# Decode attention, two gated branches on one core: one loop per engine for both branches, with branch A's sums folded and dealt out after the loops

## The chip, the core and the metric

One core of one Trainium2 chip runs the program. The metric is the device time in microseconds (us) of one execution, as the median of several runs. The engines are named as in the profile: PE (matmuls, with PEld for its weight loads), DVE (vector), ACT (scalar activations), POOL, and SP, whose queue issues nearly all the transfers of this kernel.

## What is computed

Two attention branches A and B, each with its own query weights, caches and output weights, are applied to the same `x` (two batches, one token, 512 wide) and mixed by a sigmoid gate. Each branch has 32 heads of 128 and a cache of 4096 tokens, all in float32.

```python
def _A_ref(x, k_cache, v_cache, wq, wo):        # B, Sq, D = 2, 1, 512; Hq = Hkv = 32; Sk = 4096; Dh = 128
    q = (x @ wq).reshape(B, Sq, Hq, Dh).transpose(0, 2, 1, 3)
    scores = einsum("bhqd,bhkd->bhqk", q, k_cache) * Dh ** -0.5
    p = softmax(scores, axis=-1)
    o = einsum("bhqk,bhkd->bhqd", p, v_cache)
    return o.transpose(0, 2, 1, 3).reshape(B, Sq, Hq * Dh) @ wo
...
g = sigmoid((x * gate_w).sum(-1, keepdims=True))
return g * A_ref(x, ...) + (1 - g) * B_ref(x, ...)
```

The four caches are 134 MB each and are read once. With both `wq` and both `wo` (8.4 MB each) this makes the 570 MB that the program reads.

## The kernel before

The work is cut into 32 **units**, first 16 of A and then 16 of B: a unit is four heads (a group `g` of eight) of one batch `b`. A unit's keys fill one tile of 128 partitions x 128 rows x 128 values (8.4 MB), its values another. There are two key tiles, `kt[0]` for even and `kt[1]` for odd units, and one value tile `vt`. Those three nearly fill the on-chip memory.

**Transfers.** All of them stand in SP's queue in one fixed order (L515 to L526): both `wq`, keys 0 and 1, values 0, then keys u and values u-1 in turn, then `wo` of A (into `kt[0]`), the last unit's values in three parts, and `wo` of B (into `kt[1]`) in six parts. A key transfer waits for `k_free`, which DVE gives once it has reduced the unit before in that tile (L395); a value transfer waits for `v_free`, which ACT gives once PE has used the values before (L432, L457).

**Each unit.** DVE multiplies the key tile by the spread query (L391) and reduces it to scores (L394), takes the maximum over each head (L399 to L401) and spreads the next query (L404, L405). ACT makes the exponentials (L365) into the padded weights `pr`, and their sums, one column per unit, into `lp`. PE multiplies them with the value tile (L369; 32 matmuls, which the profile shows as 64 records, since each float32 matmul is there twice). The output `vp` gathers both batches of a group. After the second unit, ACT and DVE fold its four strips into `vs[:, g]` (L452, L415), and ACT clears `vp` (L459).

**Loops and the seam between the branches.** DVE, ACT and PE each have their own loop. Before the change each runs through a loop for A, then a stretch of straight code, then a loop for B. In the straight code, the *seam*, DVE folds A's sums (`sum_of`, L467 to L470: transpose `lp`, reduce, reciprocal, times the gate), PE gathers A's eight `vs` pieces into `heads` (L473), ACT scales that into `vs[:, 0]` (L478), PE deals it out with the matrix `deal` (L482, eight matmuls) and ACT copies the result into `onA` (L485). In `deal_out`, ACT does this ahead of the exponentials of B's first unit. `deal` itself is a tile of its own, built from the identity matrix at the program's start (L313 to L320).

**The end.** After its B loop, PE projects A through `wo` of A into `most` (L497, 32 matmuls), gathers the first seven `vs` pieces of B, multiplies the last unit's weights with its values as their three parts land (`last_products`, L598), gathers the last piece, and deals B out. It then projects B, 28 rows into `most` and the last four into `qa` (L512), and adds `most` to them (L612). POOL and DVE build a second identity and a folding matrix for this in `kt[0]`, once PE has read `wo` of A there (L589 to L592). Two copies each on DVE and ACT and two small transfers end the program (L616 to L624).

PE, DVE, ACT and POOL run their instructions in the order of the code. The helper `put` adds the waits: an instruction waits for those that wrote what it reads, and for those that read or wrote what it writes. PE doesn't wait for itself.

Of the kernel before, what the change touches and what calls it, by code (L numbers as in the profile page):

```python
# [7 lines left out]
F32 = mybir.dt.float32  # L8
AF = mybir.ActivationFunctionType
# [11 lines left out]
NG = H // G  # L21
NS = SK // PH
# [119 lines left out]
def tile_gated_decode(ctx: ExitStack, tc: tile.TileContext, ins: dict, out: bass.AP):  # L142
# [9 lines left out]
    gate = {n: small.tile([P, 1], F32, name="gate" + n) for n in "AB"}  # L152
    padded = small.tile([P, NVC, B, G * VC], F32, name="pr")
    lp = small.tile([P, PH], F32, name="lp")
    slot = small.tile([P, VC], F32, name="slot")
    pick = small.tile([P, NG * B + P], F32, name="pick")
    deal = small.tile([P, B, DQ, NG, G, DQ], F32, name="deal")
    qcol = {n: small.tile([P, NG, DH // QT, B], F32, name="qcol" + n) for n in "AB"}
# [9 lines left out]
    nil = small.tile([P, 1], F32, name="nil")  # L168
# [10 lines left out]
    with tc.tile_critical():  # L179
# [10 lines left out]
        r_vs = [R() for _ in range(NG)]  # L190
# [122 lines left out]
        put("dve", lambda x: x.memset(deal, 0.0), [], [r_deal])  # L313
        for b in range(B):
            for k in range(DQ):
                piece = R()
                piece.writers = r_deal.writers[:1]
                vput("dve", lambda x: x.tensor_copy(deal[:, b, k, :, :, k], ident.rearrange(
                    "p (h g b) -> p b g h", h=G, b=B)[:, b, :NG]), [r_ident], [piece])
        r_deal.writers = piece.writers  # L320
# [4 lines left out]
        def project(n):  # L325
            i_k = place["wq", n]
            if n == "A":
                room, mark = Scratch(vt, 8 * P + D), lambda p: r_vt.readers.append(p)
            else:
                room, mark = Scratch(kt[i_k]), lambda p: None  # L330
            halves = kt[i_k].rearrange("p r d -> p (r d)").rearrange(
                "p (c i g h d) -> p c i h g d", c=KC, i=NG // STRIPS, h=G, d=DH)
            for i, t in enumerate(qa):
                put("dve", lambda x: x.memset(t, 0.0), [], [r_qa[i]])
            for c in range(KC):
                arrived("pe", ("wq", n), *((c * len(parts["wq", n]) // KC,)))
                for i, t in enumerate(qa):
                    for h in range(G):
                        put("pe", lambda x: x.matmul(t[h * QT:h * QT + B], cols[:, c], halves[:, c, i, h],  # L339
                                                     start=c == 0, stop=c == KC - 1), [r_cols, *r_kt[i_k]], [r_qa[i]])  # L340
# [10 lines left out]
            mark(put("dve", lambda x: x.tensor_copy(qcol[n], wide.rearrange("p (g k b) -> p g k b", g=NG, b=QT)[:, :, :, :B]),  # L351
                     [r_wide], [r_qcol[n]]))
            for r in r_kt[i_k]:
                r.readers += r_wide.readers

        def spread_queries(u):
            n, g, b = units[u]
            put("dve", lambda x: x.tensor_copy(qsel, qcol[n][:, g:g + 1, :, b:b + 1]), [r_qcol[n]], [r_qsel])
            put("dve", lambda x: x.transpose(q, qsel[:, 0].to_broadcast([P, DH // QT, QT])), [r_qsel], [r_q])
# [43 lines left out]
        def next_queries(n, g, b):  # L403
            at = D_.do(lambda x: x.tensor_copy(qsel, qcol[n][:, g, :, b:b + 1]))  # L404
            return D_.do(lambda x: x.transpose(q, qsel[:, 0].to_broadcast([P, DH // QT, QT])), at)  # L405

        def dve_second(nxt):
            take("dve", k_landed[1], 16)
            maxima_of(1, whole_scores(1, 0))
            return next_queries(*nxt, 0) if nxt else 0  # L410
# [7 lines left out]
        def dve_first(g, nxt, at, between=None):  # L418
# [4 lines left out]
            if between:  # L423
                between()
            maxima_of(0, at)
            next_queries(*nxt, 1)
# [27 lines left out]
        def act_first(g, col, between=None):  # L454
# [5 lines left out]
            if between:  # L460
                between()
# [3 lines left out]

        def sum_of(n):
            put("dve", lambda x: x.transpose(across, lp), [r_lp], [r_across])  # L467
            put("dve", lambda x: x.tensor_reduce(rs, across, axis=AX.X, op=ALU.add), [r_across], [r_rs])
            put("dve", lambda x: x.reciprocal(rs, rs), [], [r_rs])
            put("dve", lambda x: x.tensor_tensor(rs, rs, gate[n], op=ALU.mult), [r_gate[n]], [r_rs])  # L470

        def gather(g):
            put("pe", lambda x: x.matmul(heads, pick[:, (NG - g) * B:][:, :P], vs[:, g], start=g == 0, stop=g == NG - 1),  # L473
                [r_pick, r_vs[g]], [r_heads])

        def deal_out(n):
            t = vs[:, 0]
            put("act", lambda x: x.activation(t, heads, AF.Copy, scale=rs), [r_heads, r_rs], [r_vs[0]])  # L478
            dealt = bank[:, :B * OR].rearrange("p (b r) -> p b r", b=B)
            for b in range(B):  # L480
                for k in range(DQ):
                    put("pe", lambda x: x.matmul(dealt[:, b], deal[:, b, k].rearrange("p g h q -> p (g h q)"),  # L482
                                                 t[:, k * OR:(k + 1) * OR], start=k == 0, stop=k == DQ - 1),
                        [r_deal, r_vs[0]], [r_bank])
# [59 lines left out]
        def step(e, n, lo, hi, second, first):  # L544
            with nc.Fori(lo, hi, engines=[{"dve": mybir.EngineType.DVE, "act": mybir.EngineType.Activation}[e]]) as i:
                first(i, second(i))

        def dve_pairs(n):
            S.wait("dve", [*r_q.writers, (S.sems["dve"], S.ticks["dve"])])
            with nc.Fori(0, NG - 1, engines=[mybir.EngineType.DVE]) as i:  # L550
                nxt = n, bass.ds(i + 1, 1)
                at = dve_second(nxt)
                dve_first(i, nxt, at)

        def act_pairs():
            with nc.Fori(0, NG - 1, engines=[mybir.EngineType.Activation]) as i:
                act_second(bass.ds(i * B + 1, 1))
                act_first(i, bass.ds(i * B + B, 1))
# [23 lines left out]
        end = Scratch(kt[place["wo", "A"]]).take  # L582
        ident2, fold, onb, kept = end(P), end(QT), end(OR * B), end(D)
        totals = [end(D // OS)[:B].rearrange("b (s e) -> b s e", s=STRIPS // OS) for _ in range(OS)]
        on["B"] = onb.rearrange("p (r b) -> p r b", b=B)
        r_ident2, r_fold, r_kept, r_total = R(), R(), R(), [R(), R()]
        for r in (r_ident2, r_fold, r_kept, r_on["B"], *r_total):
            r.readers = [p for x in r_kt[place["wo", "A"]] for p in x.readers]
        put("pool", lambda x: x.memset(ident2, 0.0), [], [r_ident2])  # L589
        put("pool", lambda x: x.affine_select(out=ident2, in_=ident2, compare_op=ALU.not_equal, fill=1.0, base=0,  # L590
                                              pattern=[[-1, P]], channel_multiplier=1), [], [r_ident2])
        put("dve", lambda x: x.tensor_reduce(fold, ident2.rearrange("p (s q) -> p q s", s=STRIPS), axis=AX.X, op=ALU.add),  # L592
            [r_ident2], [r_fold])
# [5 lines left out]
        take_out(NG - 1)  # L599
        take("dve", taken)  # L600
        for a in range(1, VC):
            put("dve", lambda x: x.scalar_tensor_tensor(  # L602
                vs[:, NG - 1], vp[:, a * DH:(a + 1) * DH], slot[:, a:a + 1], vs[:, NG - 1], op0=ALU.mult, op1=ALU.add),
                [r_vs[NG - 1]] if a > 1 else [], [r_vs[NG - 1]] if a > 1 else [])
            r_vs[NG - 1].writers = [(S.sems["dve"], S.ticks["dve"])]
        gather(NG - 1)
        deal_out("B")
        project_out("B", EARLY)
        put("act", lambda x: x.activation(kept, most, AF.Copy), [r_most], [r_kept])  # L609
# [6 lines left out]
        for i, e in enumerate(("dve", "act")):  # L616
            for j in range(STRIPS // OS):
                k = (i * STRIPS // OS + j) * QT
                src = acc[i][k:k + B, :D // STRIPS]
                put(e, (lambda x: x.activation(totals[i][:, j], src, AF.Copy)) if i else  # L620
                    (lambda x: x.tensor_copy(totals[i][:, j], src)), [r_qa[i]], [r_total[i]])  # L621
            landed.append(S.dma("act" if i else "sp", out.rearrange("b o (i s e) -> (b o) i s e", i=OS, s=STRIPS // OS)[:, i],
                                totals[i], reads=[r_total[i]], slot="x"))
# [23 lines left out]
```

## Time and profile before

| | |
|---|---|
| time, median of 3 runs | 1324.59 us (1324.45 to 1324.62) |
| the profiled execution | 1324.58 us, with a span of 1322.8 us from first to last instruction |
| transfers | 570.43 MB read, mean 431 GB/s over the span |
| DVE | 1166.3 us busy, 88% of the span |
| PE | 343.3 us busy, 26%; mean granted clock 0.627 |
| ACT | 101.4 us busy, 8% |

Times in rows of the trace are in us from the span's start. A row of the timeline gives the start, the duration, the engine, the line and operation, what is written and read, and a count where instructions are merged. The square bracket says how long the engine had been idle before, and what ended that.

### The profile page before, as it was taken

What the parts mean: (1) busy time and instruction counts of PE and PEld (TensorE: products, weight loads), DVE (VectorE), ACT (ScalarE), POOL (GpSimd) and SP (SyncE); (2) the same over time, 40 slices, a digit from 0 to 9 for tenths busy, and PEclk for the clock granted to TensorE, in tenths of its full rate; (3) what the DMA queues carried; (4) which work ended last, traced back from release to release, by engine and by line L of the source; (5) the groups of instructions that cost most, each with busy time, mean ns of one, the idle gap of its engine ahead of it and who ended that gap; (6) DMA issues with size and microseconds to landing.
All of it is one profiled execution on the core that took longest, in us unless ns stands there. A gap on an engine that the chain in (4) does not pass through costs nothing. (4 is left out here: it accounts for less than half of the span.)

```text
span 1322.8 us, 6257 instructions
## 1 busy us (share of the span) xinstructions
PE 343.3 (26%) x2406; PEld 100.7 (8%) x2406; DVE 1166.3 (88%) x321; ACT 101.4 (8%) x331; POOL 1.2 (0%) x8
## 2 busy tenths in 40 slices
PE   3202222202222221222224022222212222221256
PEld 0000000000000000000002000000000000000012
DVE  2399999999999999999999899999999999999960
ACT  0000000001010000101000010100001010000100
POOL 0000000000000000000000000000000000000000
PEclk9656666556666655666665566666566666656668
DMA  9999999999999999999999999999999999999998
GB/s 412 442 414 442 442 416 442 444 414 444 442 430 428 442 442 416 442 442 416 444 442 419 438 442 434 426 440 440 420 440 440 420 442 442 426 432 442 434 420 357
DMA packets 11109, 570.53 MB, mean 431 GB/s; under 512 B 1239, under 2 KB 1243, under 8 KB 1630
## 3 DMA queue, kind: packets, MB, share of 16 engines
q1 hardware_dynamic: 11092, 570.43, 99.6%
q8 instruction: 4, 0.07, 0.0%
q14 instruction: 3, 0.02, 0.0%
q10 hardware_dynamic: 10, 0.01, 0.0%
HBM read 570.43 MB, written 0.00 MB: 431 GB/s over the span
## 5 line engine op out<-in xcount | busy, mean ns | idle before, releaser
L391 DVE TENSOR_TENSOR kt<-kt,q 128x16384 f32<-128x16384 f32 x31 | 534.0, 17226 | 56.1 <-DVEq L95 56.0
L394 DVE TENSOR_REDUCE sc<-kt 128x128 f32<-128x16384 f32 x31 | 533.8, 17220 | 1.1
L369 PE MATMUL vp<-vt,pr 128*32 128x512 f32 x2048 | 291.8, 733 | 919.3 <-PEq L95 918.5
L369 PEld LDWEIGHTS vp<-vt,pr 128*32 128x32 f32 x2048 | 80.3, 132 | 1129.3 <-issue 1126.9
L365 ACT ACTIVATE pr<-sc,nm 32x128 f32<-32x128 f32 x128 | 50.9, 398 | 160.0 <-ACTq L95 118.2
L431 ACT ACTIVATE pr<-nil 128x512 f32<-128x512 f32 x31 | 19.3, 624 | 426.4 <-ACTq L95 426.4
L452 ACT ACTIVATE vs<-vp,slot 128x128 f32 (+1 forms) x16 | 5.9, 368 | 451.6 <-ACTq L95 451.6
L339 PE MATMUL qa<-kt,cols 128*2 128x512 f32 x128 | 18.7, 741 | 22.9 <-DMA kt<-in_B_wq_dram 15.7
L365 ACT ACTIVATION_READ_ACCUMULATOR pr<-sc,nm (+1 forms) x128 | 23.5, 184 | 0.0
L350 DVE STREAM_TRANSPOSE kt<-kt 128x1024 f32<-128x1024 f32 x1 | 1.2, 1246 | 23.5 <-ACT kt L348 23.5
L415 DVE SCALAR_TENSOR_TENSOR vs<-vp,slot,vs 128x128 f32 (+1 forms) x45 | 15.8, 351 | 6.3 <-DVEq L95 5.3
L534 DVE TENSOR_REDUCE sc<-kt 128x64 f32<-128x8192 f32 x2 | 17.4, 8686 | 0.1
L533 DVE TENSOR_TENSOR kt<-kt,q 128x8192 f32<-128x8192 f32 x2 | 17.4, 8686 | 0.0
L459 ACT ACTIVATE vp<-nil 128x512 f32<-128x512 f32 x15 | 9.0, 600 | 106.6 <-ACTq L95 106.6
L621 DVE COPY kt<-qa 2x128 f32<-2x128 f32 x2 | 0.6, 280 | 17.0 <-PE qa L512 17.0
L592 DVE TENSOR_REDUCE kt<-kt 128x32 f32<-128x128 f32 x1 | 0.4, 368 | 12.8 <-POOL kt L590 12.8
L497 PE MATMUL most<-kt,onA 128*2 128x512 f32 x64 | 8.6, 698 | 9.5 <-DMA kt<-in_A_wo_dram 9.5
L399 DVE TENSOR_REDUCE rm<-sc 128x1 f32<-128x128 f32 x31 | 8.7, 282 | 2.3
L405 DVE STREAM_TRANSPOSE q<-qsel 128x128 f32<-128x128 f32 x30 | 9.3, 311 | 1.3 <-DVE qsel L404 0.3
L602 DVE SCALAR_TENSOR_TENSOR vs<-vp,slot,vs 128x128 f32<-128x128 f32 x3 | 1.1, 352 | 10.6 <-DVEq L95 10.6
L350 DVE STREAM_TRANSPOSE vt<-vt 128x1024 f32<-128x1024 f32 x1 | 1.2, 1246 | 9.4 <-ACT vt L348 9.4
L497 PE MATMUL most<-kt,kt 128*2 128x512 f32 x56 | 8.6, 779 | 2.4 <-DMA kt<-in_B_wo_dram 2.4
(68 smaller groups left out, 72.9 us busy)
## 6 DMA issues: line engine op xcount, KB each, us to landing
kt<-in_A_wq_dram SPq DMA_DIRECT2D x2, 4096.0 KB, 16.6
kt<-in_A_k_cache_dram SPq DMA_DIRECT2D x2, 4096.0 KB, 29.0
vt<-in_B_v_cache_dram SPq DMA_DIRECT2D x1, 4096.0 KB, 18.3
kt<-in_B_wo_dram SPq DMA_DIRECT2D x1, 4096.0 KB, 33.1
vt<-in_B_v_cache_dram SPq DMA_DIRECT2D x1, 3072.0 KB, 25.2
kt<-in_B_wo_dram SPq DMA_DIRECT2D x1, 2048.0 KB, 37.5
vt<-in_B_v_cache_dram SPq DMA_DIRECT2D x1, 1024.0 KB, 27.2
kt<-in_B_wo_dram SPq DMA_DIRECT2D x1, 1024.0 KB, 39.5
```

Source lines behind the costliest of these rows:

```text
L339: put("pe", lambda x: x.matmul(t[h * QT:h * QT + B], cols[:, c], halves[:, c, i, h], start=c == 0, stop=c == KC - 1), [r_cols, *r_kt[i_k]] ...
L365: do(lambda x: x.activation(padded[h, :, b, j * VC:(j + 1) * VC], s[h].rearrange("p (c a) -> p c a", a=VC), AF.Exp, bias=m[h], accum_out=l ...
L369: return x.matmul(vp[c % STRIPS * QT:(c % STRIPS + 1) * QT], padded[:, c].rearrange("p b m -> p (b m)"), vt[:, c * VC:(c + 1) * VC].rearra ...
L391: at = D_.do(lambda x: x.tensor_tensor(kt[o], kt[o], q[:, None, :].to_broadcast([P, NS, DH]), op=ALU.mult), after)
L394: at = D_.do(lambda x: x.tensor_reduce(sc[o], kt[o], axis=AX.X, op=ALU.add), at)
L405: return D_.do(lambda x: x.transpose(q, qsel[:, 0].to_broadcast([P, DH // QT, QT])), at)
L415: at = D_.do(lambda x: x.scalar_tensor_tensor(vs[:, g], vp[:, a * DH:(a + 1) * DH], slot[:, a:a + 1], vs[:, g], op0=ALU.mult, op1=ALU.add) ...
L431: return A_.do(lambda x: x.activation(padded[:, :, b], nil[:, :, None].to_broadcast([P, NVC, G * VC]), AF.Copy))
L459: A_.do(lambda x: x.activation(vp, nil.to_broadcast([P, VC * DH]), AF.Copy))
L497: put("pe", lambda x: x.matmul(most[s * QT:s * QT + B], on[n][:, r], wo[n][:, r], start=n == "A" and r < STRIPS, stop=n == "B" and r >= EA ...
L533: put("dve", lambda x: x.tensor_tensor(t, t, q[:, None, :].to_broadcast([P, NS // 2, DH]), op=ALU.mult), [r_q], [r])
L534: put("dve", lambda x: x.tensor_reduce(sc[0][:, h * NS // 2:(h + 1) * NS // 2], t, axis=AX.X, op=ALU.add), [r], [R()])
```

## The change

The two loops of each engine become one, over 15 of the 16 pairs of units; PE's runs 31 times. The straight code of the seam moves behind the loops. For this, `vs` holds 16 pieces instead of 8, so that A's sums stay unfolded until the end. `qcol` becomes one tile for both branches, so that one loop index runs through it; `lp` gets 48 columns instead of 32. The tile `deal` goes: the dealing matrix is built after the loops in the place of A's eight `vs` pieces, when PE has gathered those. The second identity is built in `q`, the folding matrix and `on["B"]` in `sc[1]`, the sum `kept` and the `totals` in B's pieces of `vs`, none of them in `kt[0]` any more. The scaled heads go to `sc[0]`. Each of the two final copies on an engine gets its own mark, so the second no longer waits for the first.

```diff
+NA = 2 * NG
...
-    deal = small.tile([P, B, DQ, NG, G, DQ], F32, name="deal")
...
-    vs = small.tile([P, NG, DH], F32, name="vs")
+    vs = small.tile([P, NA, DH], F32, name="vs")
...
-        put("dve", lambda x: x.memset(deal, 0.0), [], [r_deal])
-        for b in range(B):
-            for k in range(DQ):
-                ...
-                vput("dve", lambda x: x.tensor_copy(deal[:, b, k, :, :, k], ident.rearrange(
-                    "p (h g b) -> p b g h", h=G, b=B)[:, b, :NG]), [r_ident], [piece])
...
+        def build_deal():
+            put("dve", lambda x: x.memset(vs[:, :NG], 0.0), [], [r_deal, *r_vs[:NG]])
+            pieces = []
+            for b in range(B):
+                for k in range(DQ):
+                    pieces.append(R())
+                    pieces[-1].writers = r_deal.writers
+                    put("dve", lambda x: x.tensor_copy(deal[:, b, k, :, :, k], ident2.rearrange(
+                        "p (h g b) -> p b g h", h=G, b=B)[:, b, :NG]), [r_ident2], [pieces[-1]])
+            r_deal.writers = pieces[-1].writers
...
-        products(NU // 2)
-        dve_pairs("A")
-        act_pairs()
-        at = dve_second(("B", slice(0, 1)))
-        act_second(slice(PH // 2 - 1, PH // 2))
-        def branch_sums():
-            sum_of("A")
-            for g in range(NG):
-                r_vs[g].writers = r_rs.writers
-                gather(g)
-        dve_first(NG - 1, ("B", slice(0, 1)), at, branch_sums)
-        act_first(NG - 1, slice(0, 1), lambda: deal_out("A"))
-        products(NU // 2 - 1)
-        project_out("A", OR)
-        dve_pairs("B")
-        act_pairs()
+        products(NU - 1)
+        S.wait("dve", [*r_q.writers, (S.sems["dve"], S.ticks["dve"])])
+        with nc.Fori(0, NA - 1, engines=[mybir.EngineType.DVE]) as i:
+            nxt = bass.ds(i + 1, 1)
+            at = dve_second(nxt)
+            dve_first(i, nxt, at)
+        with nc.Fori(0, NA - 1, engines=[mybir.EngineType.Activation]) as i:
+            act_second(bass.ds(i * B + 1, 1))
+            act_first(i, bass.ds(i * B + B, 1))
         dve_second(None)
-        act_second(slice(PH // 2 - 1, PH // 2), last=True)
+        act_second(slice(NU - 1, NU), last=True)
         D_.close()
...
+        for n in "AB":
+            sum_of(n)
+        for r in (r_ident2, *r_vs[:-1]):
+            r.writers = r_rs.writers
         put("pool", lambda x: x.memset(ident2, 0.0), [], [r_ident2])
...
-        sum_of("B")
-        for g in range(NG - 1):
-            r_vs[g].writers = r_rs.writers
-            gather(g)
+        for j in range(NG):
+            gather(j)
+        build_deal()
+        deal_out("A")
+        for j in range(NG, NA - 1):
+            gather(j)
+        project_out("A", OR)
         last_products()
```

What this makes of the order of PE's matmuls is seen behind the first loop. These are PE's rows before the change, from the seam to the second dealing; `heads` is the gather, `bank` the dealing, `most` the projection, the L369 between the branches is B's loop, and a count is of matmuls in the code.

```order
L473 MATMUL heads<-vs,pick 128x128 x8
L482 MATMUL bank<-vs,deal 128x32 x8
L374 UNCONDITIONAL_BRANCH
L369 MATMUL vp<-vt,pr 32x512 x32
L374 REGISTER_ALU
L374 COMPARE_AND_BRANCH
L497 MATMUL most<-kt_86,onA 2x512 x32
L63 UNCONDITIONAL_BRANCH
L473 MATMUL heads<-vs,pick 128x128 x7
L369 MATMUL vp<-vt,pr 32x512 x32
L473 MATMUL heads<-vs,pick 128x128
L482 MATMUL bank<-vs,deal 128x32 x8
```

And these are PE's rows of the changed kernel, from its one loop to the projection of B (the line numbers are its own: 475 is the gather, 495 the dealing, 510 the projection, 361 the products).

```order
L361 MATMUL vp<-vt,pr 32x512 x32
L366 REGISTER_ALU
L366 COMPARE_AND_BRANCH
L475 MATMUL heads<-vs,pick 128x128 x8
L495 MATMUL bank<-sc_74,vs 128x32 x8
L475 MATMUL heads<-vs,pick 128x128 x7
L510 MATMUL most<-kt_82,onA 2x512 x32
L361 MATMUL vp<-vt,pr 32x512 x32
L475 MATMUL heads<-vs,pick 128x128
L495 MATMUL bank<-sc_74,vs 128x32 x8
L510 MATMUL most<-kt_83,sc_75 2x512 x28
```

A's gather and dealing have moved from ahead of B's loop to behind the one loop, ahead of A's projection; B's first gather now stands ahead of that projection too. All of it is still ahead of the last unit's products (the second L361).

On DVE the changed kernel has these rows between the last unit's scores and the final copies (468 to 471 are the sums of a branch, 579 the folding matrix, 479 and 485 the dealing matrix in `vs`).

```order
L393 TENSOR_REDUCE nm_78<-across 128x1
L468 STREAM_TRANSPOSE across<-lp 128x32
L469 TENSOR_REDUCE rm<-across 128x1
L470 RECIPROCAL rm<-rm 128x1
L471 TENSOR_TENSOR rm<-rm,few 128x1
L468 STREAM_TRANSPOSE across<-lp 128x32
L469 TENSOR_REDUCE rs<-across 128x1
L470 RECIPROCAL rs<-rs 128x1
L471 TENSOR_TENSOR rs<-rs,few 128x1
L579 TENSOR_REDUCE sc_75<-q 128x32
L479 MEMSET vs 128x1024
L485 COPY vs<-q 128x32 x8
```

Before, only one branch's sums and the folding matrix stood there; A's sums stood in the seam, and the memset and the eight copies at the program's start.

More of the change, by code (lines that the diff above doesn't have):

```diff
@@ L151, in tile_gated_decode @@
     cols = small.tile([P, KC, B], F32, name="cols")
-    gate = {n: small.tile([P, 1], F32, name="gate" + n) for n in "AB"}
+    few = small.tile([P, 8], F32, name="few")
+    gate, nil = {n: few[:, i:i + 1] for i, n in enumerate("AB")}, few[:, 2:3]
     padded = small.tile([P, NVC, B, G * VC], F32, name="pr")
-    lp = small.tile([P, PH], F32, name="lp")
+    lp = small.tile([P, PH + PH // 2], F32, name="lp")
     slot = small.tile([P, VC], F32, name="slot")
     pick = small.tile([P, NG * B + P], F32, name="pick")
-    deal = small.tile([P, B, DQ, NG, G, DQ], F32, name="deal")
-    qcol = {n: small.tile([P, NG, DH // QT, B], F32, name="qcol" + n) for n in "AB"}
+    qcol = small.tile([P, NA, DH // QT, B], F32, name="qcol")
     qsel = small.tile([P, 1, DH // QT, 1], F32, name="qsel")
@@ L189, in tile_gated_decode @@
         r_qa = [R(), R()]
-        r_vs = [R() for _ in range(NG)]
+        r_vs = [R() for _ in range(NA)]
         sem = tc.alloc_semaphore
@@ L350, in project @@
             mark(put("dve", lambda x: x.transpose(wide, qrow), r_qrow, [r_wide]))
-            mark(put("dve", lambda x: x.tensor_copy(qcol[n], wide.rearrange("p (g k b) -> p g k b", g=NG, b=QT)[:, :, :, :B]),
+            mark(put("dve", lambda x: x.tensor_copy(qcol[:, "AB".index(n) * NG:][:, :NG], wide.rearrange("p (g k b) -> p g k b", g=NG, b=QT)[:, :, :, :B]),
                      [r_wide], [r_qcol[n]]))
@@ L356, in spread_queries @@
         def spread_queries(u):
-            n, g, b = units[u]
-            put("dve", lambda x: x.tensor_copy(qsel, qcol[n][:, g:g + 1, :, b:b + 1]), [r_qcol[n]], [r_qsel])
+            j, b = divmod(u, B)
+            put("dve", lambda x: x.tensor_copy(qsel, qcol[:, j:j + 1, :, b:b + 1]), [r_qcol[units[u][0]]], [r_qsel])
             put("dve", lambda x: x.transpose(q, qsel[:, 0].to_broadcast([P, DH // QT, QT])), [r_qsel], [r_q])
@@ L409, in dve_second @@
             maxima_of(1, whole_scores(1, 0))
-            return next_queries(*nxt, 0) if nxt else 0
+            return next_queries(nxt, 0) if nxt is not None else 0
         def add_out(g, last):
@@ L422, in dve_first @@
             add_out(g, added)
-            if between:
-                between()
             maxima_of(0, at)
-            next_queries(*nxt, 1)
+            next_queries(nxt, 1)
             D_.close()
@@ L472, in gather @@
-        def gather(g):
-            put("pe", lambda x: x.matmul(heads, pick[:, (NG - g) * B:][:, :P], vs[:, g], start=g == 0, stop=g == NG - 1),
-                [r_pick, r_vs[g]], [r_heads])
+        deal = vs.rearrange("p g d -> p (g d)")[:, :NG * DH].rearrange(
+            "p (b k g h q) -> p b k g h q", b=B, k=DQ, g=NG, h=G)
+        ident2 = q
+        kept = vs.rearrange("p g d -> p (g d)")[:, NG * DH:][:, :D]
+        totals = [vs.rearrange("p g d -> p (g d)")[:, NG * DH + D:][:, i * D // OS:(i + 1) * D // OS][:B].rearrange(
+            "b (s e) -> b s e", s=STRIPS // OS) for i in range(OS)]
@@ new lines, in tile_gated_decode @@
+        sums = {"A": rm, "B": rs}
+        r_sums = {"A": r_rm, "B": r_rs}
+        on["B"] = sc[1][:, :OR * B].rearrange("p (r b) -> p r b", b=B)
+        fold = sc[1][:, OR * B:][:, :QT]
+        r_ident2, r_fold, r_kept, r_total, r_dealt = R(), R(), R(), [[R(), R()], [R(), R()]], R()
+        def sum_of(n):
+            t, r = sums[n], r_sums[n]
+            put("dve", lambda x: x.transpose(across, lp[:, "AB".index(n) * PH // 2:][:, :PH]), [r_lp], [r_across])
+            put("dve", lambda x: x.tensor_reduce(t, across, axis=AX.X, op=ALU.add), [r_across], [r])
+            put("dve", lambda x: x.reciprocal(t, t), [], [r])
+            put("dve", lambda x: x.tensor_tensor(t, t, gate[n], op=ALU.mult), [r_gate[n]], [r])
@@ new lines, in gather @@
+        def gather(j):
+            g = j % NG
+            put("pe", lambda x: x.matmul(heads, pick[:, (NG - g) * B:][:, :P], vs[:, j], start=g == 0, stop=g == NG - 1),
+                [r_pick, r_vs[j]], [r_heads])
+        def build_deal():
[8 more added lines that the diff above has]
+            r_deal.writers = pieces[-1].writers
@@ L476, in deal_out @@
         def deal_out(n):
-            t = vs[:, 0]
-            put("act", lambda x: x.activation(t, heads, AF.Copy, scale=rs), [r_heads, r_rs], [r_vs[0]])
+            t = sc[0]
+            put("act", lambda x: x.activation(t, heads, AF.Copy, scale=sums[n]), [r_heads, r_sums[n]], [r_sc])
             dealt = bank[:, :B * OR].rearrange("p (b r) -> p b r", b=B)
@@ L542, in tile_gated_decode @@
         exps(0, 0, slice(0, 1), lambda make, gives: put("act", make, [r_nm[0], r_sc, r_pad, r_lp, r_nil], [], gives))
[L544 to L553, printed above, removed]
```

49 lines of the change are left out of this document (16 added, 33 removed).

## The prediction

> **What bounds the kernel now.** I read the slices of the page first. These two rows are the busy share of the 16 DMA engines and the rate.
>
> ```profile
> DMA  9999999999999999999999999999999999999998
> GB/s 412 442 414 442 442 416 442 444 414 444 442 430 428 442 442 416 442 442 416 444 442 419 438 442 434 426 440 440 420 440 440 420 442 442 426 432 442 434 420 357
> ```
>
> The transfers fill the span from the first slice to the last but one. So engines matter in two ways only: by holding back a transfer until the queue runs dry, or by work that is still to do when the last bytes land.
>
> For the first I read the queue's own timeline around the seam (keys L231, values L239) and the time to landing.
>
> ```profile
> 580.41 0.33 SPq L231 DMA_DIRECT2D kt<-in_A_k_cache_dram  x1
> 613.92 0.33 SPq L239 DMA_DIRECT2D vt<-in_A_v_cache_dram  x1
> 657.69 0.33 SPq L231 DMA_DIRECT2D kt<-in_B_k_cache_dram  x1
> 691.73 0.33 SPq L239 DMA_DIRECT2D vt<-in_B_v_cache_dram  x1
> 734.97 0.33 SPq L231 DMA_DIRECT2D kt<-in_B_k_cache_dram  x1
> ...
> kt<-in_A_k_cache_dram SPq DMA_DIRECT2D x15, 42.6
> DVE kt L391 <- DVEq L95: 56.0, 29, 3.2
> ```
>
> A key transfer needs 42.6 us to land because two others stand ahead of it. A tile's keys are issued every 77.28 us, both ahead of the seam (580.41 to 657.69) and across it (657.69 to 734.97). DVE has time over: it waited 56.0 us in 29 waits at L391. **The seam costs the stream nothing.**
>
> For the second I read the chain of waits, and then the timeline behind 1270 us.
>
> ```profile
> 1276.21 33.05 DMA kt<-in_B_wo_dram
> ...
> 1309.31 8.70 PE most L497 x56
> ...
> 1318.03 0.61 ACT kt L609
> ```
>
> So the end is the landing of the first half of B's `wo` at 1309.3, then B's projection on PE, then the last sums. Ahead of 1309.31 PE had been waiting, and how long it waited is the room that the change may use up:
>
> ```profile
> 1279.00 0.18 ACT L365 ACTIVATION_READ_ACCUMULATOR pr<-sc,nm 32x1 f32 x1
> 1280.23 8.61 PE L497 MATMUL most<-kt,onA 128*2 128x512 f32 x64 [9.51 <-DMA kt<-in_A_wo_dram]
> 1290.93 1.83 PE L473 MATMUL heads<-vs,pick 128*128 128x128 f32 x14 [2.09 <-DVE rs L470]
> 1292.69 3.64 PE L369 MATMUL vp<-vt,pr 128*32 128x512 f32 x32
> 1297.15 3.64 PE L369 MATMUL vp<-vt,pr 128*32 128x512 f32 x32 [0.81 <-DMA vt<-in_B_v_cache_dram]
> 1303.58 3.35 PE L482 MATMUL bank<-vs,deal 128*128 128x32 f32 x16 [0.46 <-ACT vs L478]
> 1306.96 0.22 ACT L485 ACTIVATE kt<-bank 128x64 f32<-128x64 f32 x1 [3.44 <-PE bank L482]
> 1309.31 8.57 PE L497 MATMUL most<-kt,kt 128*2 128x512 f32 x56 [2.38 <-DMA kt<-in_B_wo_dram]
> ```
>
> `onB` was ready at 1307.18 (1306.96 + 0.22), so PE could have begun B's projection at about 1307.22. The **room is 2.09 us**. The last products ended at 1300.79 (1297.15 + 3.64), in a run that had waited for values to land; from there to a ready projection lie 6.43 us.
>
> **The change, part by part.** *What goes from the start.* The memset and eight copies of `deal` leave DVE.
>
> ```profile
> 13.64 0.91 DVE L313 MEMSET deal<- 128x1024 f32 x1 [0.16 <-issue]
> 14.59 0.88 DVE L318 COPY deal<-vt 128x32 f32<-128x32 f32 x8
> ...
> PE qa L339 <- DVE qa L334: 6.9, 1, 6.9
> ...
> 22.71 3.62 PE L339 MATMUL qa<-kt,cols 128*2 128x512 f32 x32 [0.24 <-DMA kt<-in_A_wq_dram]
> 42.08 9.87 PE L339 MATMUL qa<-kt,cols 128*2 128x512 f32 x64 [15.74 <-DMA kt<-in_B_wq_dram]
> ```
>
> They take 1.83 us (13.64 to 15.47), and PE's first projection waits 6.9 us for DVE, which comes to its memset behind them. But PE then waits at 22.71 for the rest of A's `wq`, and at 42.08 for B's; the queue is full behind those. I take 0.
>
> *What goes from the seam.* These rows are the seam: DVE's sums of A, PE's gather and dealing, and the next unit's products.
>
> ```profile
> 697.59 0.20 DVE L467 STREAM_TRANSPOSE across<-lp 128x32 f32<-128x32 f32 x1
> 698.25 0.16 DVE L470 TENSOR_TENSOR rs<-rs,gateA 128x1 f32<-128x1 f32 x1
> 698.46 3.78 PE L473 MATMUL heads<-vs,pick 128*128 128x128 f32 x16 [7.84 <-DVE rs L470]
> 702.70 3.62 PE L482 MATMUL bank<-vs,deal 128*128 128x32 f32 x16 [0.46 <-ACT vs L478]
> 708.32 0.18 ACT L365 ACTIVATION_READ_ACCUMULATOR pr<-sc,nm 32x1 f32 x1
> 720.16 8.78 PE L369 MATMUL vp<-vt,pr 128*32 128x512 f32 x64 [13.84 <-PEq L95]
> ...
> vt<-in_B_v_cache_dram SPq DMA_DIRECT2D x15, 28.4
> ```
>
> DVE saves 0.82 us there, and ACT's exponentials, which ended at 708.50, no longer stand behind gather and dealing (698.46 to 706.32). Both are hidden: PE began those products only at 720.16, 28.4 us after their values were issued (691.73), which is what such a transfer takes to land. The gain is 0. One index into a joint `qcol`, wider `lp` and fewer tiles leave the loop's instructions as they are: also 0.
>
> *What is added at the end.* Everything taken from the seam, and the building of the matrix, now stands between the last exponentials (1279.18) and the last products on PE. I go along that chain, with 0.05 us for each handover, as between 698.41 (698.25 + 0.16) and 698.46:
>
> - both sums on DVE, 2 x 0.82 us from 697.59 to 698.41, since every gather now waits for the second: 1280.87.
> - A's gather, 3.78 us: 1284.70. POOL's second identity and the folding matrix are made beside it.
> - the matrix, 1.83 us, which must wait for the gather, since it overwrites what the gather reads. PE is idle for it: 1286.58.
> - the dealing, 3.62 us: 1290.25. ACT's scaling lies beside the matrix, its copy into `onA` beside the next gather.
> - B's seven gathers, 14 records. They took 1.83 us at full clock (1290.93); at the seam's rate they take 14/16 x 3.78 = 3.31 us. I take the seam's rate, as PE comes here straight from dealing: 1293.56.
> - A's projection, 64 records of 128x512. The loop's products have the same count and shape and start from the same half clock. Their mean follows from the first row below, 291.8 / 32 = 9.12 us, and the other two are among the shortest and longest: 1302.68. A's `wo` has been there since 1280.23.
>
> ```profile
> L369 PE MATMUL vp<-vt,pr 128*32 128x512 f32 x2048 | 291.8, 733 | 919.3 <-PEq L95 918.5
> 526.53 10.02 PE L369 MATMUL vp<-vt,pr 128*32 128x512 f32 x64 [29.76 <-PEq L95]
> 642.49 8.37 PE L369 MATMUL vp<-vt,pr 128*32 128x512 f32 x64 [29.76 <-PEq L95]
> ```
>
> - the last products, all values landed, at full clock: 3.64 us for 32 records and about 3.43 for 32 more without a second start: 1309.75.
>
> That is 8.96 us behind 1300.79. The 2.09 us of room go first, so B's projection starts **6.87 us later**, at 1316.18, and no longer waits for a transfer. It began at half clock before and I let it do so again: 8.57 us. The last sums follow as before, but the second copy on each engine needn't wait for the first.
>
> ```profile
> 1319.58 0.59 DVE L621 COPY kt<-qa 2x128 f32<-2x128 f32 x2 [17.00 <-PE qa L512]
> ```
>
> Those two copies take 0.59 us; the independent copies of `deal` followed each other by about 0.1, which bounds the gain by 0.2. I take 0.1. **The sum is +6.77 us**, on the profiled execution's own 1324.58, which stands within 0.01 of the median: 1331.4 us.
>
> **The clock of PE** decides the large terms. The windows below show PE busy, PEld busy, then DVE, ACT, POOL, the granted clock and DMA.
>
> ```profile
> 699.70:703.10 3.40, 2.94 (x14) 2.65 (x14) 2.70 (x1) 0.37 (x1) 0.00 (x0) 0.50 0.76 328
> 703.10:706.50 3.40, 3.23 (x16) 3.09 (x15) 3.40 (x1) 0.14 (x2) 0.00 (x0) 0.50 1.36 583
> 1280.02:1283.43 3.41, 3.20 (x16) 0.55 (x20) 0.00 (x0) 0.00 (x0) 0.00 (x0) 0.50 0.98 423
> 1283.43:1286.84 3.41, 3.41 (x36) 0.76 (x32) 0.00 (x0) 0.00 (x0) 0.00 (x0) 1.00 1.00 432
> ```
>
> Gather and dealing kept PE 86% and 95% busy in the seam, and the clock stayed at 0.50; 3.2 us of projection brought it to 1.00. So I let only projections and products release the clock. The Trainium skill ("TensorE: Matmul & The Clock Gate", section "Part 1: The HAM clock gate") speaks for less: it says that about 3.4 us of sustained matmul activity, by time and not by their number, bring the full clock. By that rule A's gather alone would release it, and the sum would be 0 to 1.8 us, as in the first rival; this case's seam, 7.9 us at 0.50, doesn't bear it out.
>
> **Rivals.** *The chain runs at full clock.* If the work behind 1280.9 released the clock within A's gather, as 3.2 us of projection did, the dealing would take about 16 x 0.131 = 2.1 us at the full-clock gather's rate per record (1.83 / 14), B's gathers 1.83, A's projection 3.64 + 3.43 = 7.07 us. The last products would then end at 1304.7, 3.9 us late. Less the room, B's projection starts 1.8 us late, and if the clock held until then, it would gain those back. That gives 1324.5 to 1326.4, not slower by what a run can tell. It decides if the gathers count as work for the gate. For it: PE is busy nearly throughout. Against it: the windows above.
>
> *The stream gains.* If PE's first projection, no longer behind `deal`, let the keys be issued 1.83 us sooner and the queue had been dry, if DVE's 0.82 us in the seam counted likewise, and if the end were hidden as in the first rival, the copies' 0.1 would make 2.75 us with them, and the time 1321.8. It decides only if those issues meet an empty queue; B's `wq` landed at 42.08 and the transfers are at nine tenths in every slice.
>
> *The chain meets the clock badly.* A's projection at the longest product's 10.02 us adds 0.9, a release as late in B's projection another 0.9, and slow first instructions in the new straight code, which no row bounds, perhaps 0.5: 1333.7.
>
> *It doesn't do what it says.* If PE could pass the waiting gathers and do the products first, nothing would be late. Its rows in the changed program put the products behind A's projection, so I give this no chance of its own.
>
> **How the numbers follow.** The forecast, with the clock as in the seam, has 0.78 and its bad end 0.10; the full clock 0.10; the gain in the stream 0.02. The forecast's own lower bound is 1327.1: full-clock gathers for B (-1.5), the shortest projection (-0.75), as much in B's projection (-0.75), and a second dealing at full clock (3.35 to 2.1, -1.25). Upwards the bad end gives 1333.7. The range is 1327.1 to 1334.0; the full-clock case stays outside. A measurement of this kernel can tell about 0.2%, or 2.65 us. Slower takes the forecast and its bad end, 0.88; same the full clock, 0.10; faster 0.02.
>
> **What would show it.** In the changed kernel's profile: keys at 77.3 us through the former seam; A's gather starting near 1280.9 and the dealing near 1286.6, with the matrix between them and PE idle; A's projection from about 1293.6, after the values' first part has landed; the last products ending near 1309.8 in one run without waiting for transfers; B's projection starting near 1316.2 behind ACT's copy and not behind `wo`. The chain of waits should name ACT and PE from 1279 on, where it named the transfer. I am wrong if the last products end before about 1305, or if the granted clock is 1.00 while PE deals A out.

## The result, and the profile after

| | before | after |
|---|---|---|
| median of 8 runs each | 1324.61 us (1324.45 to 1324.94) | **1328.47 us** (1327.35 to 1329.49) |
| the profiled execution | 1324.58 us, span 1322.8 | 1327.35 us, span 1324.8 |
| PE busy, mean granted clock | 343.3 us, 0.627 | 341.9 us, 0.625 |
| DVE busy | 1166.3 us | 1166.5 us |
| read | 570.43 MB | 570.43 MB |

The ratio is 1.0029, with a 95% interval of 1.002 to 1.0038: the change makes the kernel 3.9 us slower. The profiled execution of after is the fastest of its eight. The spans of the eight lie between 1324.8 and 1327.7, so the trace below shows a mild case, only 2.0 us longer in its span than before.

These are the transfers of the even key tile ahead of the former seam and across it, in after's queue, and then DVE's wait for keys from the page's groups (L383 is what L391 was).

```profile
580.37 0.33 SPq L231 DMA_DIRECT2D kt<-in_A_k_cache_dram  x1
657.65 0.33 SPq L231 DMA_DIRECT2D kt<-in_B_k_cache_dram  x1
734.92 0.33 SPq L231 DMA_DIRECT2D kt<-in_B_k_cache_dram  x1
```

```profile
L383 DVE TENSOR_TENSOR kt<-kt,q 128x16384 f32<-128x16384 f32 x31 | 534.0, 17225 | 57.5 <-DVEq L96 57.4
```

The periods are 77.28 and 77.27 us, as before; DVE waits 57.4 us for keys, where it waited 56.0. It now waits longer by more than the 0.82 us of sums that left the seam.

The end has changed. This is PE, DVE and ACT of after behind 1280 us, from the timeline (L475 gather, L495 dealing, L510 projection, L361 products, L485 the matrix).

```profile
1280.47 3.78 PE L475 MATMUL heads<-vs,pick 128*128 128x128 f32 x16 [10.93 <-DVE rs L471]
1284.54 0.91 DVE L479 MEMSET vs<- 128x1024 f32 x1 [3.01 <-PE heads L475]
1285.48 0.88 DVE L485 COPY vs<-q 128x32 f32<-128x32 f32 x8
1286.41 1.97 PE L495 MATMUL bank<-sc,vs 128*128 128x32 f32 x16 [2.16 <-DVE vs L485]
1288.22 3.31 PE L475 MATMUL heads<-vs,pick 128*128 128x128 f32 x14
1291.46 7.12 PE L510 MATMUL most<-kt,onA 128*2 128x512 f32 x64
1298.41 7.04 PE L361 MATMUL vp<-vt,pr 128*32 128x512 f32 x64
1311.51 0.22 ACT L498 ACTIVATE sc<-bank 128x64 f32<-128x64 f32 x1 [3.31 <-PE bank L495]
1311.88 7.99 PE L510 MATMUL most<-kt,sc 128*2 128x512 f32 x56 [0.41 <-ACT sc L498]
1321.57 0.59 DVE L613 COPY vs<-qa 2x128 f32<-2x128 f32 x2 [14.31 <-PE qa L525]
```

The last products run in one piece, end at 1305.45 (before: 1300.79), and B's projection waits for ACT's copy and no longer for a transfer. The chain of waits says the same: where it named the landing of B's `wo`, it now goes along DVE, PE and ACT.

```profile
1306.91 0.36 DVE vs L592
1307.27 0.04 issue
1307.31 0.50 PE heads L475 x2
...
1308.26 3.23 PE bank L495 x16
...
1311.88 8.12 PE most L510 x56
```

### The profile page after: what moved, and what is told of

Same layout as the page of the kernel before. It is cut to its first block, busy times and chain, and to the rows that moved or that the text cites. A ratio compares the mean times of both kernels' runs of the same rounds, so it can differ in the third digit from the quotient of the medians.

```text
span 1324.8 us, 6272 instructions
## 1 busy us (share of the span) xinstructions
PE 341.9 (26%) x2406; PEld 100.6 (8%) x2406; DVE 1166.5 (88%) x321; ACT 101.4 (8%) x331; POOL 1.2 (0%) x8
## 3 DMA queue, kind: packets, MB, share of 16 engines
q1 hardware_dynamic: 11092, 570.43, 99.5%
HBM read 570.43 MB, written 0.00 MB: 431 GB/s over the span
## 5 line engine op out<-in xcount | busy, mean ns | idle before, releaser
L383 DVE TENSOR_TENSOR kt<-kt,q 128x16384 f32<-128x16384 f32 x31 | 534.0, 17225 | 57.5 <-DVEq L96 57.4
L361 PE MATMUL vp<-vt,pr 128*32 128x512 f32 x2048 | 294.2, 739 | 931.4 <-PEq L96 931.4
L361 PEld LDWEIGHTS vp<-vt,pr 128*32 128x32 f32 x2048 | 80.7, 132 | 1144.8 <-issue 1144.8
L421 ACT ACTIVATE pr<-few 128x512 f32<-128x512 f32 x31 | 19.3, 623 | 439.9 <-ACTq L96 439.9
L407 DVE SCALAR_TENSOR_TENSOR vs<-vp,slot,vs 128x128 f32 x45 | 15.8, 351 | 6.5 <-DVEq L96 5.4
L449 ACT ACTIVATE vp<-few 128x512 f32<-128x512 f32 x15 | 9.0, 600 | 104.2 <-ACTq L96 104.2
L475 PE MATMUL heads<-vs,pick 128*128 128x128 f32 x32 | 7.6, 424 | 12.8 <-DVE rs L471 10.9
L391 DVE TENSOR_REDUCE rm<-sc 128x1 f32<-128x128 f32 x31 | 8.7, 281 | 2.3
L510 PE MATMUL most<-kt,sc 128*2 128x512 f32 x56 | 8.0, 733 | 0.4 <-ACT sc L498 0.4
L475 PEld LDWEIGHTS heads<-vs,pick 128*128 128x128 f32 x32 | 6.8, 321 | 14.6 <-DVE rs L471 11.8
```

Source lines behind the costliest of these rows:

```text
L361: return x.matmul(vp[c % STRIPS * QT:(c % STRIPS + 1) * QT], padded[:, c].rearrange("p b m -> p (b m)"), vt[:, c * VC:(c + 1) * VC].rearra ...
L383: at = D_.do(lambda x: x.tensor_tensor(kt[o], kt[o], q[:, None, :].to_broadcast([P, NS, DH]), op=ALU.mult), after)
L407: at = D_.do(lambda x: x.scalar_tensor_tensor(vs[:, g], vp[:, a * DH:(a + 1) * DH], slot[:, a:a + 1], vs[:, g], op0=ALU.mult, op1=ALU.add) ...
L421: return A_.do(lambda x: x.activation(padded[:, :, b], nil[:, :, None].to_broadcast([P, NVC, G * VC]), AF.Copy))
L510: put("pe", lambda x: x.matmul(most[s * QT:s * QT + B], on[n][:, r], wo[n][:, r], start=n == "A" and r < STRIPS, stop=n == "B" and r >= EA ...
```

## The experiments

My theory was that all the lateness is the serial chain between the last exponentials and the last products, that the seam had cost nothing, and that the granted clock of PE sets the size. The rivals: the seam was worth something and the change gained it; it is the amount of PE's work behind the loop that counts, not its order; the clock plays no part. All ratios are to the kernel before, in runs on the same chip.

**1. The seam left out of the kernel before.**

```diff
+        put("dve", lambda x: x.memset(on["A"], 0.0), [], [r_on["A"]])
...
-        dve_first(NG - 1, ("B", slice(0, 1)), at, branch_sums)
-        act_first(NG - 1, slice(0, 1), lambda: deal_out("A"))
+        dve_first(NG - 1, ("B", slice(0, 1)), at)
+        act_first(NG - 1, slice(0, 1))
```

> The kernel before, with the seam's work left out: DVE's sums of A, PE's gather and dealing of A and ACT's two copies there (A's part of the output is left out, its projection still runs on zeros). Theory: the seam was hidden behind the transfers, so taking it away is worth nothing: 1324.6 +- 0.3 us. Rival: the seam held the stream back, and the change had this gain and lost it again at the end: then 0.8 us (DVE's sums) to 7 us (ACT's exponentials) less, 1323.8 or below.

Measured: 1324.70 us, ratio 1.0000 (0.9991 to 1.0009). The timeline of this run shows the exponentials after the seam and the products that use them (L370):

```profile
698.60 0.40 ACT L366 ACTIVATE pr<-sc,nm 32x128 f32<-32x128 f32 x1
...
719.91 8.49 PE L370 MATMUL vp<-vt,pr 128*32 128x512 f32 x64 [29.62 <-PEq L95]
```

ACT begins them at 698.60 instead of 706.48, and PE its products at 719.91 instead of 720.16. Nearly eight microseconds taken from ACT's path come to nothing, since the values land no sooner. The seam was hidden; there was nothing to gain there.

**2. The matrix built twice.**

```diff
         build_deal()
+        build_deal()
         deal_out("A")
```

> The changed kernel with the dealing matrix built twice over, 1.83 us more on DVE, no more work on PE. Theory: PE waits for the matrix with nothing else to do, so the time grows by about 1.9 us, to 1330.4, give or take 1 us for what the longer pause does to the clock. Rival: what holds PE there is not the matrix (ACT's scaling, or the folding matrix ahead of it), or PE has room behind it: no change, 1328.5.

Measured: 1330.72 us (1330.22 to 1331.44), ratio 1.0046 (1.0032 to 1.006): 2.25 us more than the changed kernel's median. The timeline shows PE waiting for DVE:

```profile
1280.45 3.78 PE L475 MATMUL heads<-vs,pick 128*128 128x128 f32 x16 [10.07 <-DVE rs L471]
1288.48 3.62 PE L495 MATMUL bank<-sc,vs 128*128 128x32 f32 x16 [4.25 <-DVE vs L485]
1291.92 3.33 PE L475 MATMUL heads<-vs,pick 128*128 128x128 f32 x14
1295.18 7.82 PE L510 MATMUL most<-kt,onA 128*2 128x512 f32 x64
```

PE stood idle for 4.25 us instead of 2.16, and every step of PE behind it began 2.07 us or more later than in after. The building of the matrix is on the path in full.

**3. The same work in another order.** A's gather goes right behind PE's loop, where PE idles, the identity into `sc[0]` behind ACT's loop, and the matrix ahead of the sums. The scaled heads take the identity's place in `q`, and one small activation marks the end of ACT's loop.

```diff
-        ident2 = q
+        ident2 = sc[0]
...
-            t = sc[0]
+            t = q
...
+        r_few = R()
+        put("act", lambda x: x.activation(few[:, 4:5], nil, AF.Copy), [], [r_few])
...
-        for n in "AB":
-            sum_of(n)
-        for r in (r_ident2, *r_vs[:-1]):
-            r.writers = r_rs.writers
+        r_ident2.writers = r_few.writers
+        for j in range(NG):
+            gather(j)
         put("pool", lambda x: x.memset(ident2, 0.0), [], [r_ident2])
...
+        build_deal()
+        for n in "AB":
+            sum_of(n)
...
-        for j in range(NG):
-            gather(j)
-        build_deal()
         deal_out("A")
```

> The changed kernel with the same work in another order: A's gather right behind PE's loop, POOL's second identity right behind ACT's loop, and the dealing matrix built on DVE ahead of the sums, beside ACT's last exponentials; only the dealing itself still waits for the sums. Theory: dealing of A starts near 1280.2 instead of 1286.4, so the last products end with the landing of the values near 1300.8 and all the lateness is gone: 1324.5 +- 0.5 us. Rival (it is the amount of PE work behind the loop, not the waiting, or the wider tiles slow the loop itself): 1327 or more.

Measured: 1324.83 us, ratio 1.0002 (0.9993 to 1.0011). All the lateness is gone with the same instructions at the end but for one small activation. Its timeline, with the numbers of this kernel (L593 the last fold, L510 the projections):

```profile
1269.60 2.05 PE L475 MATMUL heads<-vs,pick 128*128 128x128 f32 x16
1276.83 0.91 DVE L479 MEMSET vs<- 128x1024 f32 x1 [0.18 <-issue]
1280.28 3.59 PE L495 MATMUL bank<-q,vs 128*128 128x32 f32 x16 [8.63 <-DVE rs L470]
1294.58 7.04 PE L361 MATMUL vp<-vt,pr 128*32 128x512 f32 x64
1302.30 1.12 DVE L593 SCALAR_TENSOR_TENSOR vs<-vp,slot,vs 128x128 f32<-128x128 f32 x3 [21.62 <-DVEq L96]
1309.32 6.84 PE L510 MATMUL most<-kt,sc 128*2 128x512 f32 x48 [2.30 <-DMA kt<-in_B_wo_dram]
```

The dealing starts 6.1 us earlier than in after (1280.28 against 1286.41), beside the landing of the values, and B's projection waits for its transfer again. The amount of PE work behind the loop is therefore not what cost the time. It is that gather and matrix waited for the sums, which they don't need.

**4. Only the projection spread.** The last 12 rows of A's projection go into PE's idle times behind the last products; sums, gather and matrix stay where the change put them.

```diff
-        project_out("A", OR)
+        project_out("A", 20)
         last_products()
+        project_out("A", 20, 28)
...
         gather(NA - 1)
+        project_out("A", 28, 30)
         deal_out("B")
+        project_out("A", 30, OR)
         project_out("B", EARLY)
```

> The changed kernel with the same work, but the last 12 of the 32 rows of A's projection moved behind the last products: 8 into the 1.9 us in which PE waits for the last fold, 2 ahead of the last dealing and 2 behind it. Theory (lateness is PE's serial time ahead of the last products): these end 2.6 us earlier and PE's idle time takes the rows for nothing: 1328.5 - 2.6 = 1325.9, and by the clock of the single execution 1325.0 to 1326.5. Rival (the end is set by the amount of PE work, idle time is not to be had): 1328 or more.

Measured: 1324.58 us (1324.24 to 1325.2), ratio 1.0001 (0.9992 to 1.001). This is 3.9 us less than the changed kernel, 1.3 more than I had expected for the rows moved, and below the range that I had given. The timeline shows why:

```profile
1295.97 7.05 PE L361 MATMUL vp<-vt,pr 128*32 128x512 f32 x64
1302.84 1.90 PE L510 MATMUL most<-kt,onA 128*2 128x512 f32 x16
1306.24 1.97 PE L495 MATMUL bank<-sc,vs 128*128 128x32 f32 x16
1309.12 3.61 PE L510 MATMUL most<-kt,sc 128*2 128x512 f32 x32
1313.97 1.90 PE L510 MATMUL most<-kt,sc 128*2 128x512 f32 x16 [1.23 <-DMA kt<-in_B_wo_dram]
```

The rows fill the pause in which the clock used to fall. The last dealing takes 1.97 us instead of 3.23, and B's projection runs 32 records in 3.61 us and then waits for the transfer. The path is the landing of B's `wo` again. This is also why none of these versions beats the kernel before: this one, the one of experiment 3 and the last of experiment 5 all wait for that landing, as their rows of B's projection show, and their medians lie within 0.3 us of the kernel before.

**5. The clock.** PE's idle 10.9 us ahead of A's gather were filled with matmuls whose results nobody uses.

```diff
+        for _ in range(44):
+            put("pe", lambda x: x.matmul(acc[0], pick[:, :P], vs[:, :STRIPS].rearrange("p g d -> p (g d)"), start=True, stop=True),
+                [r_pick], [r_qa[0]])
         for j in range(NG):
             gather(j)
```

> The changed kernel with 44 matmuls more on PE, whose results nobody uses, between the end of its loop and A's gather, where PE was idle for 10.9 us. They add work and keep the granted clock at 1.00. Theory (the size of the lateness is the clock's): gather of A about 2.1 us instead of 3.78, dealing 2.0, gather of B 1.83 instead of 3.31, projection of A 6.9 to 7.1; the last products end near 1302.5 and B's projection starts at the landing of its weights or within 0.5 us of it: 1324.4 to 1325.4, with a spread of the runs under 0.5 us. Rival (the lateness is the order of the steps alone, whatever the clock): 1328.5, as the changed kernel.

Measured: 1353.38 us, ratio 1.0218 (1.0204 to 1.0232). As a test this failed: I had sized the filler by the products' record of 0.107 us, and these took four times that.

```profile
1269.54 38.03 PE L582 MATMUL qa<-vs,pick 128*128 128x512 f32 x88
1307.41 1.95 PE L475 MATMUL heads<-vs,pick 128*128 128x128 f32 x16
1311.51 2.86 PE L495 MATMUL bank<-sc,vs 128*128 128x32 f32 x16 [2.16 <-DVE vs L485]
1314.18 3.33 PE L475 MATMUL heads<-vs,pick 128*128 128x128 f32 x14
```

The price of the gather at full clock can be read all the same, 1.95 us, and that the clock was lost again during the dealing. The next two use 12 such matmuls; the second adds 2 in the pause for the matrix.

> The changed kernel with 12 matmuls more on PE ahead of A's gather, in the 10.9 us in which PE was idle (the 44 of the run before took 0.43 us per record, since they used all columns, and held PE until 1307). They should end near 1279.9, ahead of the sums. Theory (the clock sets the size): A's gather at 1.95 us instead of 3.78, so 1.8 us less at least; whether the full clock outlasts the pause for the matrix is open, so the dealing takes 2.0 to 2.9 and B's gather 1.8 to 3.3 us: 1325.0 to 1326.9. Rival (the clock has no part in it): 1328.5.

Measured: 1325.20 us (1324.89 to 1327.1), ratio 1.0007 (0.9998 to 1.0016). The profiled execution is one of three above 1326, with 1326.61 us:

```profile
1280.51 2.05 PE L475 MATMUL heads<-vs,pick 128*128 128x128 f32 x16
1284.71 2.56 PE L495 MATMUL bank<-sc,vs 128*128 128x32 f32 x16 [2.15 <-DVE vs L485]
1287.09 3.33 PE L475 MATMUL heads<-vs,pick 128*128 128x128 f32 x14
1290.35 8.20 PE L510 MATMUL most<-kt,onA 128*2 128x512 f32 x64
```

The full clock did not outlast the pause for the matrix: B's gather took 3.33 us, as at half clock.

In the last run `fill(n)` stands for n such matmuls, from other pieces of `vs` than those that the matrix overwrites.

```diff
+        fill(12)
         for j in range(NG):
             gather(j)
         build_deal()
+        fill(2)
         deal_out("A")
```

> The same, with 2 more matmuls in the pause in which PE waits for the matrix. Theory: PE is then never idle long enough to lose the full clock ahead of the last products; A's gather 1.95, dealing 2.0, B's gather 1.9 and A's projection 7.1 us, the last products end near 1303.0 and B's projection is ready near 1309.4, just when its weights land: 1324.6 to 1325.4. Rival (dealing loses the clock by itself, however busy PE is around it): B's gather stays at 3.3 us and the time at 1326 or more.

Measured: 1324.82 us (1324.35 to 1325.09), ratio 1.0002 (0.9993 to 1.0011).

```profile
1285.32 1.97 PE L495 MATMUL bank<-sc,vs 128*128 128x32 f32 x16 [0.44 <-DVE vs L485]
1287.12 1.81 PE L475 MATMUL heads<-vs,pick 128*128 128x128 f32 x14
1288.86 7.05 PE L510 MATMUL most<-kt,onA 128*2 128x512 f32 x64
1295.73 7.05 PE L361 MATMUL vp<-vt,pr 128*32 128x512 f32 x64
1309.59 8.53 PE L510 MATMUL most<-kt,sc 128*2 128x512 f32 x56 [2.05 <-DMA kt<-in_B_wo_dram]
```

With more work on PE the chain is shorter: the last products end at 1302.78, and B's projection waits for its transfer. The order of the change alone costs nothing when PE keeps its clock. Both parts are needed for the lateness: the serial order, and the half clock in it. Without the first (experiment 3) or the second (this run) the time is that of the kernel before.

## Why the prediction was right, and where its size was off

The direction, the place and the serial path held; the clock along that path did not. +6.77 us were forecast and +3.86 measured at the median, so the forecast was 1.75 times the measured size. Step by step, with the profiled execution of after beside it:

| step | predicted | in the trace |
|---|---|---|
| start and seam | 0 | 0 (experiment 1, and equal key periods) |
| A's gather starts | 1280.92 | 1280.47 |
| A's gather | 3.78 | 3.78 |
| pause for the matrix | 1.93 | 2.16 |
| dealing of A, until the next gather | 3.62 | 1.81 |
| B's first gathers, until the projection | 3.31 | 3.24 |
| projection of A, until the products | 9.12 | 6.95 |
| last products | 7.07 | 7.04 |
| from there to B's projection | 6.43 | 6.43 |
| projection of B | 8.57 | 7.99 |
| second copies without a wait | -0.1 | 0 (0.59 us for two, as before) |

The start is early because the last exponentials ended 0.36 us sooner and the sums with their handovers took 1.65 us instead of 1.74. The profiled span is 2.0 us longer than before, 4.8 us less than the forecast. Three terms make nearly all of that: dealing (-1.8), A's projection (-2.2) and B's (-0.6). All three are the clock.

**The step that failed** is the one that said: "So I let only projections and products release the clock." The seam had led me there, where gather and dealing ran 7.9 us at 0.50. These windows of after show PE busy, PEld busy, then DVE, ACT, POOL, the granted clock and DMA; they are cut where the clock changes. In all nine traces of this case these changes lie whole multiples of 3.413 us apart.

```profile
1281.43:1284.84 3.41, 2.82 (x14) 2.52 (x12) 0.40 (x2) 0.37 (x1) 0.00 (x0) 0.50 1.04 452
1284.85:1288.26 3.41, 1.85 (x17) 1.85 (x17) 1.47 (x9) 0.00 (x0) 0.00 (x0) 1.00 0.98 420
1288.26:1291.67 3.41, 3.41 (x20) 3.08 (x23) 0.00 (x0) 0.22 (x1) 0.00 (x0) 0.50 1.01 430
1291.67:1295.08 3.41, 3.41 (x36) 0.76 (x32) 0.00 (x0) 0.00 (x0) 0.00 (x0) 1.00 0.94 404
```

A window with 2.82 us of gather was followed by a full clock, one with the pause and the dealing by half, and one full of B's gather by full again. So the gather does release the clock, the dealing fell at full clock for its most part by that, and A's projection found the clock full already. A granted clock of 1.00 while PE deals A out was one of the two signs by which the prediction would have been wrong, and it came. The other, last products that end before about 1305, was missed by 0.45 us (1305.45). In the run with the matrix built twice the windows lay otherwise:

```profile
1279.72:1283.13 3.41, 2.68 (x12) 2.68 (x13) 0.94 (x5) 0.00 (x0) 0.50 (x2) 0.50 1.04 452
1283.13:1286.54 3.41, 1.10 (x6) 0.81 (x4) 1.78 (x9) 0.37 (x1) 0.00 (x0) 0.50 0.93 404
...
1289.95:1293.37 3.42, 3.42 (x18) 3.42 (x18) 0.00 (x0) 0.22 (x1) 0.00 (x0) 0.50 1.03 446
1293.37:1296.78 3.41, 3.41 (x17) 1.84 (x20) 0.00 (x0) 0.00 (x0) 0.00 (x0) 0.50 0.89 380
```

The same 3.78 us of gather put 2.68 us into one window and 1.10 into the next, and the clock stayed at half. The dealing there took 3.62 us, as I had forecast. Between 2.68 and 2.82 us of gather in a 3.41 us window lies what releases the clock, as far as these two go; the seam had some 2.5 us of gather in a window (699.70 to 702.24). The products have a sharper edge near that. The nine traces hold 493 windows at half clock with nothing but the loop's products on PE; all with up to 2.60 us of them were followed by half clock (the longest from 757.48, with the matrix built twice), and all from 2.62 us on by full (the shortest from 873.84, in the kernel before). At full clock, windows with up to 1.37 us of products lost it and those from 1.39 us on kept it.

Half of my rule stands: no window mostly of dealing released the clock. The third window above was busy throughout, with 1.97 us of dealing and 1.45 of gather, and half clock followed. For the gather the seam was one case of two, and I took it for a rule about the kind of work.

The rule of the Trainium skill that I had set aside ("TensorE: Matmul & The Clock Gate", section "Part 1: The HAM clock gate") was nearer to the truth on the gather: it counts activity in a free-running window, whatever the matmuls. Its reading as time alone is not borne out by the dealing, which held PE 95% busy in a window of the seam without a release, nor by the window above that was busy throughout.

My first rival, a clock released within A's gather with 1324.5 to 1326.4 us, came about in part. In after the dealing took 1.81 us and A's projection 6.95, near the rival's 2.1 and 7.07, and the last products ended at 1305.45, where the rival had 1304.7 and the forecast 1309.75. What the rival did not count is that the clock falls again behind the pause for the matrix: B's first gathers took 3.24 us and not 1.83. With the clock held from A's gather on, in the last run of experiment 5, the last products ended at 1302.78 and the time was 1324.82, inside the rival's range; there A's gather ran at full clock too.

That the measured time lies in the forecast's range is in part luck. The lower bound of 1327.1 took the time off B's gathers, both projections and the second dealing. In the trace of after, B's gathers and the second dealing ran at about the forecast's prices; more than half of what was saved came from A's dealing at full clock, which no bound held, and from a projection of A shorter than the shortest that I had allowed (6.95 us against 8.37).

The eight runs of after reach from 1327.35 to 1329.49. That they differ by where the windows lie is argued from these traces; only one run of after was profiled, so it is not shown for the others.

## What to carry to other kernels

Work that is moved to the end of a kernel bound by transfers costs its serial chain less the room at the end. Both are read in the timeline behind the last big transfer's issue, and the room is the wait that names the transfer. Such a chain is shortened first by its order: what doesn't need the latest result (here gather and matrix) goes ahead of it, and rows that nobody waits for go into the pauses, where they also hold PE's clock. When a duration was seen at one clock only, look at where its window lay before making a rule of it. Here 14 unused matmuls in PE's pauses took the changed kernel from 1328.5 to 1324.8 us.

## What was not expected of the hardware

In experiment 3 POOL's `affine_select` over 128x128 stood beside DVE's multiplication of a key tile. It took 16.49 us there, against 295 ns in the kernel before, and ended 0.15 us behind the multiplication.

```profile
1241.27 17.23 DVE L383 TENSOR_TENSOR kt<-kt,q 128x16384 f32<-128x16384 f32 x1 [1.53 <-DVEq L96]
1242.16 16.49 POOL L577 TENSOR_SCALAR_AFFINE_SELECT sc<-sc 128x128 f32<-128x128 f32 x1
```

The Trainium skill ("SBUF — State Buffer", section "SBUF: two separate sides") tells of an access path that DVE and POOL share and that one of them locks for a whole instruction, which agrees with this row. Nobody waited for it here.

The filler of experiment 5 has the products' moving size of 128x512 but a stationary side of 128 columns instead of 32. Its records took 38.03 / 88 = 0.43 us at a granted clock of 1.00, where the products take 7.04 / 64 = 0.11: a product's record costs a quarter of the filler's. The products differ from the filler in the number of stationary columns and in going to four strips of `vp` in turn, and no run here shows which of the two makes the quarter.
